# Sliding-window attention into a per-sentence expert MLP: the gate chain placed ahead of the masks, and four loads placed elsewhere in the queue

## The chip, the cores and the metric

The kernel runs on one core of a Trainium2 chip. Times are device microseconds of one execution. The kernel before was timed three times, and its median is the number to compare with. One more execution was taken by the hardware profiler, and all rows of a profile that are shown below come from it.

## The reference

```python
def reference(q, k, v, w_gate, w1, w2):          # q, k, v: 8 x 8 x 576 x 64
    scores = q @ k.T / 8                          # per batch and head, 576 x 576
    mask = (rel >= 0) & (rel < 64)                # rel = query position - key position
    attn = softmax(where(mask, scores, -1e9)) @ v
    x = attn, heads side by side                  # 8 x 576 x 512
    logits = x.mean(axis=1) @ w_gate              # 8 x 8: one row of logits per batch
    e = argmax(logits); g = softmax(logits)[e]
    out[b] = g * (relu(x[b] @ w1[e]) @ w2[e])     # w1: 512 x 1024, w2: 1024 x 512
```

Each batch (a sentence of 576 positions) picks one expert out of eight by the mean of its attention output, so the expert's weights can be fetched only when the attention of the whole batch is done.

## The kernel before, in words

The work is cut into 16 units `u`. A unit is four heads of one batch, so batch `b` has the units 2b and 2b+1. A unit passes these stages, each a helper function:

- `load_qk(u)` (L208) issues two DMAs on GpSimd's queue, which also cast q and k from float32 to bfloat16. `load_v(b)` (L219) issues v of a whole batch on SyncE's queue, behind a small GpSimd instruction.
- `transpose_qk(u, which)` (L329) transposes q (0) or k (1) on TensorE; ScalarE or VectorE copies the result out of PSUM.
- `scores(u, c)` (L366) makes a third of the score blocks on TensorE (tile `sp`). ScalarE takes exp into `pt` (L389), and VectorE multiplies `pt` by a 0/1 mask in place (L391).
- `cast_part(u, part)` (L305) copies v on VectorE: "whole" casts it to `va`, "low" and "high" copy `va`, shifted by half a block, into `vb`.
- `values(u, s)` (L398) multiplies `pt` with `va` and `vb` on TensorE (L413), and VectorE normalizes into `x` (L427, L429). It reads all three thirds of the masked `pt`.
- `transpose_x(u)` (L441) transposes `x` (L450); ScalarE copies it to `xT` and sums over positions on the way (L458). VectorE adds the gate's partial sums `gpart` (L476, L480).
- `gate(b)` (L486) is one small matmul `gl` (L488), then on VectorE `glog`, the maximum, its index and `eidx` (L492 to L500). GpSimd reads `eidx` into a register (L505), and only then can `load_w1(b)` (L526) and `load_w2(b)` (L538) be issued on its queue. `gate_weight(b)` (L510) makes the softmax weight, by which ScalarE scales `hT`.
- `expert_up(b, ft)` (L545) is one tile of x times w1 (L557), with relu on ScalarE into `hT` (L561). `expert_down(b, mt)` (L565) is a tile of hT times w2 (L571, L580), copied out on VectorE or ScalarE to `ob` and stored on SyncE's queue.

Every engine runs its instructions in the order in which the program emits them, so the order is written by hand. Units 0 to 3 are emitted one after the other (L686 to L757). From `t = 4` on, a loop (L759) runs a step for each unit: transposed x of unit t-1, scores and values of unit t, the transposes of unit t+1, and in between `experts(pace)`, which takes the next tiles of an endless list of expert tiles of earlier batches by a running budget, about eight times a step. In each even step the gate of batch t/2 - 1 is worked out by `next_gate()`: after the first `experts(pace)` in step 4, after the second in the steps 6 to 14. It issues w1, then q and k of unit t+4 (in the steps 6, 8 and 10), then w2, then v. In the odd steps `load_qk(t + 4)` is issued at the step's start.

q and k have six buffers each, w1 and w2 two each, PSUM has four buffers of two banks in one rotation, and `pt` has six.

Of the kernel before, what the change touches and what calls it, by code (L numbers as in the profile page):

```python
# [14 lines left out]
ALU = mybir.AluOpType  # L15
# [141 lines left out]
def kernel(  # L157
# [10 lines left out]
    nc = tc.nc  # L168
# [6 lines left out]
    NU = 2 * B  # L175
# [4 lines left out]
    def P(ins):  # L180
        tc.keep_in_program_order(ins)
        return ins
# [18 lines left out]
    kv = k.rearrange("b h s d -> (b h s d)").rearrange(  # L201
        "(u s r c) -> u r s c", u=NU, s=2, c=NT * D)
# [2 lines left out]

    qk_tiles = {}

    def load_qk(u):  # L208
        qn = qkn.tile([128, 2, NT * D], BF16, tag="qn")
        kn = qkn.tile([128, 2, NT * D], BF16, tag="kn")  # L210
        P(nc.gpsimd.dma_start(out=qn, in_=qv[u]))
        if u == 0:
            load_v(0)
        P(nc.gpsimd.dma_start(out=kn, in_=kv[u]))
        qk_tiles[u] = (qn, kn)

    v_tiles = {}
# [1 line left out]
    def load_v(b, behind=None):  # L219
        vn = vpool.tile([128, NM, D], FP32, tag="vn")  # L220
        if behind is None:

            P(nc.gpsimd.memset(vn[:, 0, 0:1], 0.0))
        else:

            P(nc.gpsimd.tensor_copy(out=vn[:, 0, 0:1], in_=behind))
        P(nc.sync.dma_start(out=vn, in_=vv[b]))
        v_tiles[b] = vn
# [37 lines left out]
    for (half, e, own) in ((0, 0, True), (1, 0, False), (0, 1, False), (1, 1, True)):  # L266
        sl = par[64 * half:64 * half + 64, e, :]
        if own:

            P(nc.gpsimd.affine_select(  # L270
                out=sl, in_=sl, compare_op=ALU.is_ge, fill=OUT, base=0,
                pattern=[[1, 64]], channel_multiplier=-1))
        else:

            P(nc.gpsimd.affine_select(
                out=sl, in_=sl, compare_op=ALU.is_ge, fill=OUT, base=-1,
                pattern=[[-1, 64]], channel_multiplier=1))
    outside = const.tile([128, 3, 6, 64], BF16)
    for c in range(3):
        P(nc.vector.tensor_copy(  # L280
            out=outside[:, c].rearrange("p (g e) w -> p g e w", e=2),
            in_=par[:, None, :, :].broadcast_to([128, 3, 2, 64])))
    P(nc.vector.memset(outside[64:128, 0, 0, :], OUT))
    P(nc.vector.memset(outside[0:64, 1, 3, :], OUT))
    masks = const.tile([128, 3, 2, 6, 64], FP16)
# [13 lines left out]
    def copy_on(eng, out, in_):  # L299
        if eng is nc.scalar:  # L300
            P(nc.scalar.copy(out=out, in_=in_))  # L301
        else:
            P(eng.tensor_copy(out=out, in_=in_))  # L303

    def cast_part(u, part, eng=None):  # L305
        b, qd = divmod(u, 2)
        i = b % 2
        vn = v_tiles[b]
        lo, hi = qd * HM, qd * HM + HM
        l1 = max(lo, 1)  # L310

        src = vn if eng is nc.gpsimd else va[i]
        eng = eng or nc.vector
        if part == "whole":
            copy_on(eng, va[i][:, lo:hi, 0:D], vn[:, lo:hi, :])
        elif part == "low":
            copy_on(eng, vb[i][0:64, lo:hi, 0:D], src[0:64, lo:hi, 0:D])
        else:
            copy_on(eng, vb[i][64:128, l1:hi, 0:D], src[64:128, l1 - 1:hi - 1, 0:D])

    def cast_v(u):
        for part in ("whole", "low", "high"):
            cast_part(u, part)

    qt_tiles, kt_tiles, pt_tiles, x_tiles, xt_tiles = {}, {}, {}, {}, {}
# [37 lines left out]
                rhs=outside[:, c].rearrange("p g w -> p (g w)"), start=True, stop=False))  # L363
        sp_ps[u, c] = sp

    def scores(u, c):  # L366
        qT, kT = qt_tiles[u], kt_tiles[u]
        masked = (u, c) in sp_ps
        if not masked:
            sp_ps[u, c] = psum.tile([128, 2, 512], FP32, tag="ps", name="sp")  # L370
        sp = sp_ps[u, c]

        def mm(s, half, kblk, qblk, n):
            P(nc.tensor.matmul(  # L374
                out=sp[64 * half:64 * half + 64, s,
                       64 * (qblk - 6 * c):64 * (qblk - 6 * c) + n],
                lhsT=kT[64 * s:64 * s + 64, ts(kblk, 64)],
                rhs=qT[64 * s:64 * s + 64, 64 * qblk:64 * qblk + n],
                start=not masked, stop=not masked or kblk >= g0 + 4,
                tile_position=(64 * s, 64 * half)))  # L380

        g0 = 6 * c
        for s in range(2):
            mm(s, 1, 1 if c == 0 else g0 - 1, g0, 64)
        for g in range(g0, g0 + 6):
            for s in range(2):
                mm(s, g % 2, g, g, 128 if g < g0 + 5 else 64)
        pt = ptp.tile([128, 2, 384], FP16, tag="pt")
        P(nc.scalar.activation(out=pt, in_=sp[:, :, 0:384], func=AF.Exp, scale=scale))  # L389
        if not masked:  # L390
            P(nc.vector.tensor_tensor(  # L391
                out=pt, in0=pt, in1=masks[:, c].rearrange("p s g w -> p s (g w)"),
                op=ALU.mult))
        pt_tiles[u, c] = pt

    op_ps = {}

# [37 lines left out]
    def x_chunk(b, kb):  # L435

        if b == 0:
            return slice(128 * kb, 128 * kb + 128)
        return slice(256 * (kb // 2) + kb % 2, 256 * (kb // 2 + 1), 2)

    def transpose_x(u, chunks=(0, 1), parts=True, eng=None):  # L441
        b, qd = divmod(u, 2)
        if qd == 0 and chunks[0] == 0:
            xt_tiles[b] = xtp.tile([128, KB, S], FP16, tag="xT", name=f"xT{b}")
        x, xT = x_tiles[b], xt_tiles[b]
        tp = psum.tile([128, 2, 1024], FP16, tag="ps")
        for kl in chunks:
            kb = 2 * qd + kl
            for jj in range(5):
                P(nc.tensor.transpose(  # L450
                    out=tp[:, kl, ts(jj, 128)],
                    in_=x[:, jj, x_chunk(b, kb)], identity=identh))
        for kl in chunks:
            kb = 2 * qd + kl
            if eng is not None:
                copy_on(eng, xT[:, kb, :], tp[:, kl, 0:S])
                continue
            P(nc.scalar.activation(  # L458
                out=xT[:, kb, :], in_=tp[:, kl, 0:S], func=AF.Copy,
                accum_out=pooled[:, b, kb:kb + 1]))  # L460
        if parts:
            for kl in chunks:
                gate_parts(b, 2 * qd + kl)
# [74 lines left out]
    def load_w2(b):  # L538
        P(nc.gpsimd.dma_start(
            out=weights[b][1].rearrange("p (g i) d -> p g i d", i=4),  # L540
            in_=w2e[experts_of[b]].squeeze(0)))
# [94 lines left out]
    def experts(amount):  # L636

        acc[0] += amount
        while acc[0] > 0.0:
            nxt = next(stream, None)  # L640
            if nxt is None:
                return
            nxt[0]()
            halves[0] = False
            acc[0] -= nxt[1]

            free[0] = nxt[2]

    per_step = (8 * 1.0 + 4 * 1.7 + 0.9) / 2
    START = 3  # L650
# [45 lines left out]
    for c in range(3):  # L696
        scores(0, c)
# [3 lines left out]
    leave_qk(1, 1, A)  # L701
    load_qk(3)
    load_qk(4)
    cast_v(0)
    cast_v(1)
    for c in range(3):
# [15 lines left out]
    gate(0)  # L722
    load_w1(0)
    load_w2(0)
    load_qk(5)
    load_v(2, w1_parts()[:, 0, 0, 0:1])
    load_qk(6)
    load_v(3)
# [24 lines left out]
    values(3, 1)  # L753
    transpose_qk(4, 0)
    transpose_qk(4, 1)
    experts(2.0)
    transpose_x(3)  # L757

    for t in range(START + 1, NU + LAG):  # L759
        pace = per_step / 8.0 * 0.96  # L760
        on, prev, ahead = t < NU, START + 1 < t <= NU, t + 1 < NU

        def next_gate():
            b = t // 2 - 1
            gate(b)
            load_w1(b)
            if START + 1 < t < NU - 4:
                load_qk(t + 4)
            load_w2(b)
            if t // 2 + 2 < B:  # L770
                load_v(t // 2 + 2)
            if t == START + 1:
                load_qk(7)

        for u in [8, 9] if t == 5 else [t + 4] if t % 2 == 1 else []:
            if u < NU:
                load_qk(u)
        if prev:
            transpose_x(t - 1)
        if ahead and t > 5:  # L780
            cast_part(t + 1, "whole")
        if on:
            scores(t, 0)
            scores(t, 1)
        experts(pace)
        if t == START + 1 or t == NU:
            next_gate()
        if t == NU:
            gate_weight(B - 1)
            okc = row_check()  # L790
        if ahead and t > 5:
            cast_part(t + 1, "low")
            cast_part(t + 1, "high")
        experts(pace)
        if START + 1 < t < NU and t % 2 == 0:
            next_gate()
        if on:
            scores(t, 2)
        if START < t < NU and t % 2 == 0:
            gate_weight(t // 2 - 1)  # L800
        if t == START + 1:
            cast_v(t)
        experts(pace)
        experts(pace)

        if ahead:
            transpose_qk(t + 1, 1, leave=False)
            leave_qk(t + 1, 1, free[0])
        if on:
            values(t, 0)  # L810
        halves[0] = on
        experts(pace)
        experts(pace)
        if ahead:
            transpose_qk(t + 1, 0)
        if on:
            values(t, 1)
        halves[0] = on
        if t in (4, 5):
            cast_v(t + 1)  # L820
        if t == NU:
            row_flag(okc)
        experts(pace)
        experts(pace)
# [38 lines left out]
```

## Time and profile before

| | us |
|---|---|
| median of 3 runs | 231.01 |
| lowest and highest run | 228.78, 231.4 |
| profiled execution | 227.06 |
| its span, first to last instruction | 225.2 |
| TensorE busy | 201.0 (89%) |
| VectorE busy | 128.9 (57%) |
| ScalarE busy | 134.5 (60%) |
| GpSimd busy | 37.8 (17%) |

PE is TensorE (PEld its weight loads), DVE is VectorE, ACT is ScalarE, POOL is GpSimd and SP is SyncE. A row of the timeline has the start, the duration, the engine, the line of the kernel, the operation, and output and inputs by the program's names; `x8` counts instructions merged into the row. What stands in brackets is how long the engine was idle before it, and what ended that. A row of the chain that ended last has start, duration and name alone. TensorE's idle time comes from few places: the first 14 us, in which q and k arrive, some waits in between, and the end, where the last tiles are copied and stored.

### The profile page before, as it was taken

Reading aid. Unit: us, or ns where it says so; the run is one execution under the profiler, and the core shown is the slowest. Engines: PE = TensorE matmul, PEld = TensorE weight load, DVE = VectorE, ACT = ScalarE, POOL = GpSimd, SP = SyncE. Lnnn points to the kernel's source line nnn. Section 1 sums busy time; section 2 is a strip of 40 time slices with the busy share of each in tenths; the row PEclk is TensorE's granted clock in tenths of the full one; section 3 lists DMA queues with packets and bytes.
Section 4 is the critical chain, followed back from the end, with each engine's and each line's share of the span. In section 5 each row is a group of like instructions: output and inputs, shape, how many; then the busy total and the mean of one; then the engine's idle time right before and its main releaser. Section 6 shows DMA issues by size and latency. Waiting matters only on the chain.

```text
span 225.2 us, 6993 instructions
## 1 busy us (share of the span) xinstructions
PE 201.0 (89%) x3011; PEld 142.6 (63%) x3012; DVE 128.9 (57%) x310; ACT 134.5 (60%) x220; POOL 37.8 (17%) x67
## 2 busy tenths in 40 slices
PE   7869879988799996999999998999999998999980
PEld 2436758845488655866687656865687567659630
DVE  2639695576856865575775668475948572511130
ACT  2366795962669664695769474977397457416410
POOL 7160360036000150007000610020002000200000
PEclk9979699999999999999999999999999999999996
DMA  5999899999999999998999999999941995499142
GB/s 74 241 256 248 140 187 220 245 252 221 230 234 253 274 215 237 230 271 165 225 235 243 259 212 242 234 281 205 226 147 10 184 224 175 53 223 243 74 148 69
DMA packets 29910, 45.64 MB, mean 203 GB/s; under 512 B 2480, under 2 KB 21936, under 8 KB 29872
## 3 DMA queue, kind: packets, MB, share of 16 engines
q0 software_dynamic: 13840, 26.22, 64.7%
q1 hardware_dynamic: 15232, 18.88, 27.6%
q8 instruction: 25, 0.41, 0.7%
q10 hardware_dynamic: 800, 0.03, 0.2%
q14 instruction: 13, 0.11, 0.1%
HBM read 61.90 MB, written 9.44 MB: 317 GB/s over the span
## 4 chain that ended last, share of the span: by engine, by line
PE 59%; DMA 16%; ACT 14%; DVE 4%; issue 2%; POOL 1%; POOLq 0%
PE php L557 24%; PE pso L571 18%; DMA w1t<-in_moe_w_dram 11%; PE tp L334 6%; ACT pt L389 5%; ACT xT L458 5%; DMA kn<-in_k_dram 4%; PE op L413 4%; ACT hT L561 4%; PE pso L580 2%; PE tp L450 1%; PE sp L374 1%; PE sp L361 1%; DVE vb L303 1%; DVE pt L391 1%
## 5 line engine op out<-in xcount | busy, mean ns | idle before, releaser
L557 PE MATMUL php<-xT,w1t 128*128 128x288 f16 x512 | 69.8, 287 | 5.1 <-DMA w1t<-in_moe_w_dram 4.3
L561 ACT ACTIVATE hT<-php,gatew 128x576 f16<-128x576 f32 x64 | 47.0, 745 | 31.6 <-PE php L557 31.6
L557 PEld LDWEIGHTS <-w1t 128*128 128x128 f16 x512 | 55.7, 115 | 12.6 <-DMA w1t<-in_moe_w_dram 6.0
L571 PE MATMUL pso<-w2t,hT 128*128 128x512 f16 x256 | 60.5, 380 | 1.0 <-ACT hT L561 0.9
L571 PEld LDWEIGHTS <-hT 128*128 128x128 f16 x256 | 23.3, 98 | 27.7 <-issue 1.8
L389 ACT ACTIVATE pt<-sp 128x768 f16<-128x768 f32 x48 | 36.6, 820 | 7.1 <-PE sp L374 7.1
L303 DVE COPY ob<-pso 128x512 f32<-128x512 f32 x24 | 16.5, 689 | 24.2 <-PE pso L571 24.1
L534 POOL DMA_DIRECT2D w1t<-in_moe_w_dram x7 | 5.0, 716 | 138.1 <-PE tp L334 62.8
L391 DVE TENSOR_TENSOR pt<-pt,masks 128x768 f16<-128x768 f16 x42 | 23.2, 555 | 7.5 <-ACT pt L389 6.4
L429 DVE TENSOR_TENSOR x<-op,linv 128x640 f16<-128x640 f32 x32 | 26.4, 824 | 1.1
L347 ACT COPY dst<-tp 128x1152 bf16<-128x1152 bf16 x16 | 18.0, 1122 | 14.1 <-PE tp L334 13.8
L458 ACT ACTIVATE xT<-tp 128x576 f16<-128x576 f16 x28 | 17.9, 646 | 6.2 <-PE tp L450 6.2
L413 PE MATMUL op<-vb,pt 128*64 128x65 f16 x320 | 16.0, 195 | 2.6 <-DVE vb L303 1.4
L413 PEld LDWEIGHTS <-pt 128*64 128x64 f16 x640 | 13.6, 111 | 4.8 <-issue 3.0
L374 PE MATMUL sp<-dst 64*64 64x128 bf16 (+1 forms) x672 | 14.1, 218 | 2.4 <-ACT dst L301 1.1
L413 PE MATMUL op<-va,pt 128*64 128x65 f16 x320 | 15.8, 195 | 0.0
L480 DVE SCALAR_TENSOR_TENSOR gpart<-wg,pooled,gpart 128x8 f32<-128x8 f32 x21 | 4.7, 226 | 19.3 <-ACT xT L458 19.2
L374 PEld LDWEIGHTS <-dst 64*64 64x64 bf16 x672 | 10.6, 110 | 7.5 <-issue 3.0
L427 DVE RECIPROCAL linv<-op 128x10 f32<-128x10 f32 x32 | 6.9, 217 | 14.4 <-PE op L413 14.3
L303 DVE COPY vb<-va 64x1152 f16<-64x1152 f16 (+1 forms) x32 | 14.9, 465 | 0.5
L303 DVE CAST va<-vn 128x1152 f16<-128x1152 f32 x16 | 12.4, 778 | 3.9 <-DMA vn<-in_v_dram 3.9
L334 PE MATMUL tp<-ident,kn 128*64 128x128 bf16 x288 | 11.5, 227 | 1.7 <-DMA kn<-in_k_dram 1.6
(71 smaller groups left out, 179.5 us busy)
## 6 DMA issues: line engine op xcount, KB each, us to landing
w2t<-in_moe_w_dram POOLq DMA_DIRECT2D x8, 1024.0 KB, 16.4
out_dram<-ob SPq DMA_DIRECT2D x32, 256.0 KB, 7.5
w1t<-in_moe_w_dram POOLq DMA_DIRECT2D x7, 1024.0 KB, 8.8
qn<-in_q_dram POOLq DMA_DIRECT2D x16, 288.0 KB, 13.7
kn<-in_k_dram POOLq DMA_DIRECT2D x16, 288.0 KB, 14.8
w1t<-in_moe_w_dram POOLq DMA_DIRECT2D x2, 512.0 KB, 6.4
out_dram<-ob SPq DMA_DIRECT2D x16, 64.0 KB, 7.5
vn<-in_v_dram SPq DMA_DIRECT2D x8, 0.2 KB, 19.7
```

The source lines that it names most:

```text
L303: P(eng.tensor_copy(out=out, in_=in_))
L334: P(nc.tensor.transpose(out=tp[64 * s:64 * s + 64, ts(t, 128)], in_=src[:, s, ts(t, D)], identity=ident, tile_position=(0, 64 * s)))
L347: P(nc.scalar.copy(out=dst.rearrange("p (x r t) -> p x r t", x=2, t=NT), in_=view))
L374: P(nc.tensor.matmul(out=sp[64 * half:64 * half + 64, s, 64 * (qblk - 6 * c):64 * (qblk - 6 * c) + n], lhsT=kT[64 * s:64 * s + 64, ts(kblk ...
L389: P(nc.scalar.activation(out=pt, in_=sp[:, :, 0:384], func=AF.Exp, scale=scale))
L391: P(nc.vector.tensor_tensor(out=pt, in0=pt, in1=masks[:, c].rearrange("p s g w -> p s (g w)"), op=ALU.mult))
L413: P(nc.tensor.matmul(out=op[64 * half:64 * half + 64, xx, 65 * jj:65 * jj + 65], lhsT=pt[:, s, 64 * (g % 6):64 * (g % 6) + 64], rhs=win, s ...
L429: P(nc.vector.tensor_tensor(out=x[:, :, h0 * D:(h0 + 2) * D].rearrange("p j (x c) -> p x j c", x=2), in0=view[:, :, :, 0:64], in1=li[:, :, ...
L458: P(nc.scalar.activation(out=xT[:, kb, :], in_=tp[:, kl, 0:S], func=AF.Copy, accum_out=pooled[:, b, kb:kb + 1]))
L557: P(nc.tensor.matmul(out=php[:, sc, 0:288], lhsT=w1t[:, kb, cols], rhs=xT[:, kb, ts(sc, 288)], start=(kb == 0), stop=(kb == KB - 1)))
L561: P(nc.scalar.activation(out=hT[:, ft].rearrange("p (sc s) -> p sc s", sc=2), in_=php[:, :, 0:288], func=AF.Relu, scale=gatew[:, b:b + 1]))
L571: P(nc.tensor.matmul(out=pso[:, 0, :], lhsT=hT[:, fb, ts(mt, 128)], rhs=w2t[:, fb, :], start=(fb == 0), stop=(fb == FB - 1)))
```

## The change

It has four parts.

1. In the even steps from 4 on (`gated`), `scores(t, 0)` and `scores(t, 1)` leave out the mask multiplication. The gate follows directly after the first `experts(pace)` (in step 4 ahead of it), then come the two mask multiplications (`mask_out`), and in the steps 6 to 14 the "whole" cast of the next unit's v, which stood ahead of the scores before. In step 16 the order stays as it was.
2. `transpose_x(3)` stands one expert tile earlier.
3. From step 6 on, q and k are loaded for unit t+3, no longer t+4; unit 8 is loaded in step 5 alone, and unit 9 in step 6, behind w1.
4. q of unit 5 is issued ahead of the first gate, behind q and k of unit 4. Its k stays behind w1 and w2 of batch 0.

```diff
-    def load_qk(u):
+    def load_qk(u, q=True, k=True):
+        if not q:
+            P(nc.gpsimd.dma_start(out=qk_tiles[u][1], in_=kv[u]))
+            return
...
-        P(nc.gpsimd.dma_start(out=kn, in_=kv[u]))
+        if k:
+            P(nc.gpsimd.dma_start(out=kn, in_=kv[u]))
...
-    def scores(u, c):
+    def scores(u, c, mask=True):
...
-        if not masked:
-            P(nc.vector.tensor_tensor(
-                out=pt, in0=pt, in1=masks[:, c].rearrange("p s g w -> p s (g w)"),
-                op=ALU.mult))
         pt_tiles[u, c] = pt
+        if mask and not masked:
+            mask_out(u, c)
+
+    def mask_out(u, c):
+        pt = pt_tiles[u, c]
+        P(nc.vector.tensor_tensor(
+            out=pt, in0=pt, in1=masks[:, c].rearrange("p s g w -> p s (g w)"),
+            op=ALU.mult))
...
     load_qk(4)
+    load_qk(5, k=False)
...
-    load_qk(5)
+    load_qk(5, q=False)
...
-    experts(2.0)
+    experts(1.0)
     transpose_x(3)
+    experts(1.0)
...
-            if START + 1 < t < NU - 4:
-                load_qk(t + 4)
+            if START + 1 < t < NU - 3:
+                load_qk(t + 3)
...
-        for u in [8, 9] if t == 5 else [t + 4] if t % 2 == 1 else []:
-            if u < NU:
-                load_qk(u)
+        gated = START < t <= NU and t % 2 == 0
+        if t % 2 == 1 and t + 3 < NU:
+            load_qk(t + 3)
         if prev:
             transpose_x(t - 1)
-        if ahead and t > 5:
+        if ahead and t > 5 and not gated:
             cast_part(t + 1, "whole")
         if on:
-            scores(t, 0)
-            scores(t, 1)
-        experts(pace)
-        if t == START + 1 or t == NU:
+            scores(t, 0, not gated)
+            scores(t, 1, not gated)
+        if t > START + 1:
+            experts(pace)
+        if gated:
+
             next_gate()
+            if on:
+                mask_out(t, 0)
+                mask_out(t, 1)
+        if t == START + 1:
+            experts(pace)
...
         if ahead and t > 5:
+            if gated:
+                cast_part(t + 1, "whole")
             cast_part(t + 1, "low")
             cast_part(t + 1, "high")
         experts(pace)
-        if START + 1 < t < NU and t % 2 == 0:
-            next_gate()
         if on:
             scores(t, 2)
-        if START < t < NU and t % 2 == 0:
+        if gated and on:
             gate_weight(t // 2 - 1)
```

## The prediction

> **What bounds the kernel now.** I read the page first, then what TensorE waits for, then the chain that ended last, then the order of single instructions in the even steps, because the diff touches these alone.
>
> ```profile
> span 225.2 us, 6993 instructions
> DMA  5999899999999999998999999999941995499142
> w1t<-in_moe_w_dram POOLq DMA_DIRECT2D x7, 1024.0 KB, 8.8
> kn<-in_k_dram POOLq DMA_DIRECT2D x16, 288.0 KB, 14.8
> ```
>
> The second row gives the tenths of DMA business in 40 slices: from slice 2 to about slice 30 the DMA engines hardly rest. The last two are issue rows, with KB each and the median us from issue to landing: 8.8 for w1, 14.8 for a k. In TensorE's timeline two tiles of the first expert product stand long for w1 (start, duration, in brackets the wait before):
>
> ```profile
> 60.49 1.17 PE L557 MATMUL php<-xT,w1t 128*128 128x288 f16 x8 [1.66 <-DMA w1t<-in_moe_w_dram]
> 86.37 1.17 PE L557 MATMUL php<-xT,w1t 128*128 128x288 f16 x8 [2.19 <-DMA w1t<-in_moe_w_dram]
> ```
>
> They are batches 1 and 2, loaded by the gates of steps 4 and 6. From the chain that ended last:
>
> ```profile
> 48.61 11.83 DMA w1t<-in_moe_w_dram
> ...
> 77.78 8.55 DMA w1t<-in_moe_w_dram
> ```
>
> So VectorE's gate chain (glog, max, index, eidx) sets when GpSimd may issue w1, here 48.61 and 77.78, and in these two places TensorE ends up waiting for the landing. Together that is 1.66 + 2.19 = 3.85 us, and it is what the change can win. Batch 3 shows no such wait, but it has nothing to spare:
>
> ```profile
> 110.88 2.15 PE L557 MATMUL php<-xT,w1t 128*128 128x288 f16 x16 [0.22 <-ACT pt L389]
> ```
>
> Its w1 was issued at 101.90 (row below), and 101.90 + 8.8 = 110.7.
>
> **The gate chain and the masks.** Step 8 shows how every gated step from 6 to 14 runs now:
>
> ```profile
> 96.04 2.28 PE L557 MATMUL php<-xT,w1t 128*128 128x288 f16 x16
> 97.16 0.23 DVE L480 SCALAR_TENSOR_TENSOR gpart<-wg,pooled,gpart 128x8 f32<-128x8 f32 x1 [0.40 <-ACT xT L458]
> 97.30 0.75 DVE L303 CAST va<-vn 128x1152 f16<-128x1152 f32 x1
> 97.97 1.15 DVE L391 TENSOR_TENSOR pt<-pt,masks 128x768 f16<-128x768 f16 x2
> 98.15 0.28 PE L488 MATMUL gl<-gpart,onesf 128*128 128x8 f32 x2
> 98.58 0.36 PE L374 MATMUL sp<-dst 64*64 64x64 bf16 x14
> 99.03 0.92 DVE L303 COPY vb<-va 64x1152 f16<-64x1152 f16 x2
> 99.21 1.89 PE L571 MATMUL pso<-w2t,hT 128*128 128x512 f16 x8 [0.27 <-ACT hT L561]
> 99.98 0.17 DVE L492 COPY glog<-gl 128x8 f32<-128x8 f32 x1
> 100.81 0.55 DVE L391 TENSOR_TENSOR pt<-pt,masks 128x768 f16<-128x768 f16 x1
> 101.02 0.69 PE L334 MATMUL tp<-ident,kn 128*64 128x128 bf16 x18
> 101.90 0.72 POOL L534 DMA_DIRECT2D w1t<-in_moe_w_dram  x1 [19.78 <-PE tp L334]
> ```
>
> VectorE does the cast, two masks and the vb copies (97.30 to 99.95) while the gate's sums have been ready since 97.16 + 0.23 = 97.39. After the change, TensorE's gl comes one expert tile (half of the 2.28 us row) earlier and is then held by gpart. How fast gl follows gpart, step 4 shows:
>
> ```profile
> 44.90 0.23 DVE L480 SCALAR_TENSOR_TENSOR gpart<-wg,pooled,gpart 128x8 f32<-128x8 f32 x1 [0.41 <-ACT xT L458]
> 45.27 0.36 PE L488 MATMUL gl<-gpart,onesf 128*128 128x8 f32 x2 [0.32 <-DVE gpart L480]
> ```
>
> 0.14 us, and 0.36 to its end. So gl runs 97.53 to 97.89, glog starts at 97.93, and w1 is issued 1.92 behind that (99.98 to 101.90): 99.85 instead of 101.90, 2.05 us sooner.
>
> *Step 6, batch 2.* 2.05 sooner turns 86.37 into 84.32; TensorE gets there at 86.37 - 2.19 = 84.18, plus the delay worked out next (about 0.5), so the wait is gone: 2.19 won, bounds 1.5 and 2.19. *Step 4, batch 1.* The two masks no longer stand ahead of glog (97.97 to 99.03, 1.06 us), and transpose_x(3) is moved ahead by one tile of 1.1 us, of which I count 0.7, because it may then have to wait for the norm of unit 3. That is 1.76 against a wait of 1.66: all of it won, bounds 1.06 (the masks alone) and 1.66.
>
> *What the masks cost.* The chain ends where mask 2 starts now, 0.83 behind glog: 98.76. Then come masks 0 and 1 (1.06), the cast (0.67, 97.30 to 97.97), the vb copies (0.95), and mask 2 (0.55): it ends at 101.99 instead of 101.36, 0.63 later, because VectorE idles while gl runs. Moreover the w1, q, k and w2 issues on GpSimd, 0.72 each from 99.85 on, now lie beside the cast and the copies, as in step 4 today:
>
> ```profile
> 49.68 0.95 DVE L303 CAST va<-vn 128x1152 f16<-128x1152 f32 x1 [0.35 <-DMA vn<-in_v_dram]
> 50.66 1.13 DVE L303 COPY vb<-va 64x1152 f16<-64x1152 f16 x2
> ```
>
> 0.95 and 1.13 against 0.75 and 0.92: 0.41 more. So mask 2 is 0.63 to 1.04 us late. Who waits: the value product of the same step, which follows the k transposes on TensorE. I take 0.53 us from the start of these and some 13 of 20 matmuls (0.2) before the third score block is read; that is an estimate from the 0.69 of the row, whose end overlaps with the next. Margins, step by step, mask 2 against these transposes:
>
> ```profile
> 76.41 0.55 DVE L391 TENSOR_TENSOR pt<-pt,masks 128x768 f16<-128x768 f16 x1
> 76.78 0.69 PE L334 MATMUL tp<-ident,kn 128*64 128x128 bf16 x18
> ...
> 124.81 0.55 DVE L391 TENSOR_TENSOR pt<-pt,masks 128x768 f16<-128x768 f16 x1
> 125.02 0.69 PE L334 MATMUL tp<-ident,kn 128*64 128x128 bf16 x18
> ...
> 148.82 0.55 DVE L391 TENSOR_TENSOR pt<-pt,masks 128x768 f16<-128x768 f16 x1
> 150.33 0.69 PE L334 MATMUL tp<-ident,kn 128*64 128x128 bf16 x18
> ...
> 171.83 0.55 DVE L391 TENSOR_TENSOR pt<-pt,masks 128x768 f16<-128x768 f16 x1
> 172.28 0.69 PE L334 MATMUL tp<-ident,kn 128*64 128x128 bf16 x18
> ```
>
> The slack is transposes + 0.73 - end of mask 2: 0.55 in step 6, 0.39 in steps 8 and 10, 1.69 in step 12, 0.63 in step 14. With 1.04 the new waits are 0.5 + 0.65 + 0.65 + 0 + 0.4 = 2.2 us, with 0.63 they are 0.1 + 0.25 + 0.25 + 0 + 0 = 0.6. Holding TensorE at gl costs about 0.4 a step, but what follows in step 8 waits for ScalarE anyway (0.27) and the score product after gl stood 0.15 (98.43 to 98.58), so some 0.1 a step is left: 0.4 in all over steps 4 to 14. Sum of the costs 1.0 to 2.6; I take 2.0, nearer the upper end, since the issues do fall on the casts.
>
> **The q and k loads.** One pair (2 x 288 KB) moves from ahead of w1 of batch 2 to behind it, and each later pair one step back. A step is about 12 us (half of 101.02 to 125.02), so some 24 us are left to a load, and a k lands in 14.8. I cost it at nothing: the two steps of work between issue and use hide it. Without that cover, a landing later than 24 us would hold the transposes by the rest. The DMA queue ahead of w1 gets shorter. **q of unit 5** goes into the queue right behind k of unit 4, ahead of the first gate. Its place is where the DMA engines rest (last two columns: DMA share, GB/s):
>
> ```profile
> 26.00:27.00 1.00, 1.00 (x13) 1.00 (x11) 0.65 (x3) 1.00 (x2) 0.63 (x1) 0.50 0.29 54
> 27.00:28.00 1.00, 1.00 (x27) 0.90 (x27) 0.86 (x3) 1.00 (x3) 1.00 (x3) 0.89 0.43 22
> 28.00:29.00 1.00, 0.95 (x24) 0.66 (x19) 1.00 (x3) 1.00 (x2) 1.00 (x2) 1.00 0.52 65
> ```
>
> Of 3 us 1.8 are idle. At w1's pace (1024 KB in 8.8 us, latency included) 288 KB take at most 2.5, so up to 0.7 may be left over to delay the first w1; on the other side v and k behind it may land sooner, which I bound by the same 0.7. I take 0: the rest of the transfer is hidden by the idle stretch.
>
> **The sum** on the profiled execution: 3.85 - 2.0 = 1.85 won, span 223.35; its own time was 227.06 (span + 1.86), so 225.2. The median of the runs shown is 231.01, 3.95 above that execution. What the longer runs spend is not shown. If it were late w1 for batches 3 to 7, which land with 0.2 us to spare, an issue 2 us earlier would win part of it: bounds 0 and 3.95, I take 1.0. Median after: 231.01 - 1.85 - 1.0 = **228.2 us**. A measurement of this kernel can tell about 2% (4.6 us) from no change, so this counts as within.
>
> **Rivals.** *Slower: w1's issue collides with the casts.* Where it is issued just ahead of va and vb, in step 4, it takes 11.83 to land instead of 8.8. The change puts every issue from step 6 on there. With 11.83, w1 of batch 2 lands at 77.78 - 2.05 + 11.83 = 87.6 against 84.7 (2.9 wait instead of 2.19), batch 3 at 111.7 against 111.5. Sum: -1.66 + 0.7 + 0.2 + 2.0 = +1.25, no slack won: 232.3. It ends slower from a landing time of 10.8 us on. For it: the step-4 rows. Against: that transfer also had v and q/k transfers beside it. [...]
>
> *More than forecast.* Casts aren't slowed and the slack pays: 231.01 - 3.85 + 1.0 - 2.0 = 226.2, down to 224 with all of the 3.95 bar 0.2. For it: the bare margins of batch 3. *w1 lands no sooner*, because the DMA row stays at 9 and the queue is served in order: nothing won, 0.6 of the costs hidden in the waits that stay, 231.0 + 1.4 = 232.4. Against it: fewer bytes stand ahead.
>
> **Chances.** Forecast 0.5 (226.5 to 230.5), more 0.25, collision 0.15, no sooner 0.1. Range 224 to 232.8, from the large gain to just beyond the two losses. Faster by over 2% takes less than 226.4: most of the second case and a little of the first, 0.25. Slower by over 2% takes more than 235.6, which needs collisions at several later batches as well: 0.10. Within: 0.65.
>
> **What would show it.** Right: no wait for w1 at batches 1 and 2; glog straight behind gl in steps 6 to 14; w1 issued about 2 us sooner against the step; new waits of the value product for mask 2 of 0.2 to 0.7 us in steps 6, 8, 10, 14. Wrong: w1 landings of 11 us or more in these steps (collision), waits for w1 still there, a first w1 landing later than now, or waits for q or k.

## The result, and the profile after

| | before | after |
|---|---|---|
| median of 12 runs, us | 228.90 | 226.69 |
| lowest and highest run | 228.16, 231.40 | 225.42, 230.22 |
| profiled execution, us | 227.06 | 226.77 |
| its span, us | 225.2 | 224.5 |

The ratio is 0.988, with a 95% interval from 0.983 to 0.992. It compares means, and the two longest runs of after (229.47 and 230.22), over 1.5% above its shortest, are left out as slow. The forecast of 228.2 against 231.01 was also a ratio of 0.988. So the kernel became about 2.8 us faster (1.7 to 3.9), which is within 2%. The two profiled executions differ by only 0.3 us in their own times, because that of before was shorter than all 12 timed runs of its kernel. What follows therefore reads stretches of the profiles and not their totals.

From the page of the profile of the changed kernel:

```profile
span 224.5 us, 6988 instructions
PE 200.5 (89%) x3011; PEld 141.5 (63%) x3012; DVE 129.2 (58%) x310; ACT 134.1 (60%) x220; POOL 37.9 (17%) x67
w1t<-in_moe_w_dram POOLq DMA_DIRECT2D x7, 1024.0 KB, 9.2
kn<-in_k_dram POOLq DMA_DIRECT2D x16, 288.0 KB, 12.8
```

TensorE's busy time has hardly moved (201.0 before). The gain lies in its waits. In its timeline, the first tiles of batches 0, 1 and 2:

```profile
32.90 2.15 PE L565 MATMUL php<-xT,w1t 128*128 128x288 f16 x16 [1.11 <-DMA w1t<-in_moe_w_dram]
...
60.28 1.14 PE L565 MATMUL php<-xT,w1t 128*128 128x288 f16 x8 [0.67 <-DVE ob L307]
...
84.25 1.14 PE L565 MATMUL php<-xT,w1t 128*128 128x288 f16 x8
```

Both waits for w1 that the prediction counted, 1.66 and 2.19, are gone. Batch 1 now waits 0.67 for VectorE's copy `ob`; its w1 landed at 59.75 (tile view below), 0.53 ahead of the tile. Batch 0 waits 1.11 for its w1, where the profile before has this:

```profile
31.68 2.15 PE L557 MATMUL php<-xT,w1t 128*128 128x288 f16 x16 [0.48 <-DMA w1t<-in_moe_w_dram]
```

The start of each batch's first tile cuts the span into stretches. They are the measure used below, in us from the first expert tile:

| kernel | first tile | batch 0 to 1 | 1 to 2 | 2 to 7 |
|---|---|---|---|---|
| before | 31.68 | 28.81 | 25.88 | 116.20 |
| after | 32.90 | 27.38 | 23.97 | 117.15 |
| difference | +1.22 | -1.43 | -1.91 | +0.95 |

What is left to the span's -0.7 is +0.5 behind batch 7, where I followed nothing up. A second profile of the changed kernel, further down, doesn't repeat this: its span is 223.5, its first tile starts at 32.56, and behind batch 7 it is 0.15 shorter than before.

Step 8 of the changed kernel, in the timeline:

```profile
93.97 1.17 PE L565 MATMUL php<-xT,w1t 128*128 128x288 f16 x8
95.09 0.23 DVE L488 SCALAR_TENSOR_TENSOR gpart<-wg,pooled,gpart 128x8 f32<-128x8 f32 x1 [0.41 <-ACT xT L466]
95.46 0.36 PE L496 MATMUL gl<-gpart,onesf 128*128 128x8 f32 x2 [0.32 <-DVE gpart L488]
95.86 0.17 DVE L500 COPY glog<-gl 128x8 f32<-128x8 f32 x1 [0.54 <-PE gl L496]
96.68 1.02 DVE L400 TENSOR_TENSOR pt<-pt,masks 128x768 f16<-128x768 f16 x2
97.61 0.75 DVE L307 CAST va<-vn 128x1152 f16<-128x1152 f32 x1
97.97 0.72 POOL L542 DMA_DIRECT2D w1t<-in_moe_w_dram  x1 [19.02 <-DVE pt L400]
98.40 1.28 DVE L307 COPY vb<-va 64x1152 f16<-64x1152 f16 x2
99.00 0.69 PE L338 MATMUL tp<-ident,kn 128*64 128x128 bf16 x18
99.72 0.56 DVE L400 TENSOR_TENSOR pt<-pt,masks 128x768 f16<-128x768 f16 x1
100.33 0.22 PE L421 MATMUL op<-vb,pt 128*64 128x65 f16 x1 [0.42 <-DVE pt L400]
```

The chain runs as the prediction laid it out: gl 0.14 behind gpart, glog 0.04 behind gl, w1 2.11 behind glog (1.92 before). Against the step's first expert tile w1 is issued 97.97 - 93.97 = 4.00 later. Before it was 101.90 - 96.04 = 5.86, so the issue is 1.86 us sooner (2.05 was forecast). The last row is the new wait for mask 2.

### The profile page after: what moved, and what is told of

It is laid out like the page before. It is cut to its first block, busy times and chain, and to the rows that moved or that the text cites. A ratio compares the mean times of both kernels' runs of the same rounds, so it can differ in the third digit from the quotient of the medians.

```text
span 224.5 us, 6988 instructions
## 1 busy us (share of the span) xinstructions
PE 200.5 (89%) x3011; PEld 141.5 (63%) x3012; DVE 129.2 (58%) x310; ACT 134.1 (60%) x220; POOL 37.9 (17%) x67
## 3 DMA queue, kind: packets, MB, share of 16 engines
q1 hardware_dynamic: 15232, 18.88, 27.8%
## 4 chain that ended last, share of the span: by engine, by line
PE 63%; DVE 13%; ACT 10%; DMA 7%; issue 3%; POOL 1%; POOLq 0%
PE php L565 25%; PE pso L579 20%; PE tp L338 5%; ACT xT L466 5%; DMA kn<-in_k_dram 5%; PE op L421 4%; PE pso L588 3%; DVE vb L307 3%; DMA w1t<-in_moe_w_dram 3%; DVE pt L400 2%; ACT hT L569 2%; DVE x L437 2%; PE sp L378 2%; ACT pt L393 2%; PE tp L458 2%
## 5 line engine op out<-in xcount | busy, mean ns | idle before, releaser
L579 PEld LDWEIGHTS <-hT 128*128 128x128 f16 x256 | 23.2, 98 | 25.8 <-issue 1.2
L307 DVE COPY ob<-pso 128x512 f32<-128x512 f32 x24 | 16.5, 688 | 24.4 <-PE pso L579 24.3
L351 ACT COPY dst<-tp 128x1152 bf16<-128x1152 bf16 x16 | 17.9, 1120 | 14.6 <-PE tp L338 14.2
L400 DVE TENSOR_TENSOR pt<-pt,masks 128x768 f16<-128x768 f16 x42 | 22.7, 555 | 3.9 <-ACT pt L393 2.8
L421 PE MATMUL op<-vb,pt 128*64 128x65 f16 x320 | 17.1, 195 | 3.6 <-DVE pt L400 2.0
L421 PEld LDWEIGHTS <-pt 128*64 128x64 f16 x640 | 14.2, 110 | 6.5 <-DVE pt L400 2.4
L421 PE MATMUL op<-va,pt 128*64 128x65 f16 x320 | 16.8, 196 | 0.0
L307 DVE COPY vb<-va 64x1152 f16<-64x1152 f16 (+1 forms) x32 | 16.0, 500 | 0.7
L378 PE MATMUL sp<-dst 64*64 64x128 bf16 (+1 forms) x672 | 13.6, 213 | 1.6 <-ACT dst L305 0.8
L378 PEld LDWEIGHTS <-dst 64*64 64x64 bf16 x672 | 9.8, 107 | 8.1 <-issue 4.1
```

Of the source, the lines that this page charges most:

```text
L351: P(nc.scalar.copy(out=dst.rearrange("p (x r t) -> p x r t", x=2, t=NT), in_=view))
L378: P(nc.tensor.matmul(out=sp[64 * half:64 * half + 64, s, 64 * (qblk - 6 * c):64 * (qblk - 6 * c) + n], lhsT=kT[64 * s:64 * s + 64, ts(kblk ...
L400: P(nc.vector.tensor_tensor(out=pt, in0=pt, in1=masks[:, c].rearrange("p s g w -> p s (g w)"), op=ALU.mult))
L421: P(nc.tensor.matmul(out=op[64 * half:64 * half + 64, xx, 65 * jj:65 * jj + 65], lhsT=pt[:, s, 64 * (g % 6):64 * (g % 6) + 64], rhs=win, s ...
L579: P(nc.tensor.matmul(out=pso[:, 0, :], lhsT=hT[:, fb, ts(mt, 128)], rhs=w2t[:, fb, :], start=(fb == 0), stop=(fb == FB - 1)))
```

## The experiments

Every diff is against the changed kernel. "After" and "before" are the two kernels of the case, and ratios are to before. In five of these profiles TensorE runs at half clock (granted 0.50) for some 3.5 us around the start of the first expert tile or just behind it. A star marks a stretch lengthened by this, and the last section returns to it.

**The gate order alone.** The three other parts are undone.

```diff
-    load_qk(5, k=False)
...
-    load_qk(5, q=False)
+    load_qk(5)
...
-    experts(1.0)
+    experts(2.0)
     transpose_x(3)
-    experts(1.0)
...
-                load_qk(t + 3)
+                load_qk(t + 4)
...
-        if t % 2 == 1 and t + 3 < NU:
-            load_qk(t + 3)
+        for u in [8, 9] if t == 5 else [t + 4] if t % 2 == 1 else []:
+            if u < NU:
+                load_qk(u)
```

> Only the gate chain ahead of the masks; the loads and transpose_x(3) as before. Theory (w1 is issued sooner because VectorE's chain no longer stands behind masks and casts): the wait for w1 at batch 1 shrinks from 1.66 us to 0.6 or less (transpose_x(3) is not earlier here), that at batch 2 goes; new waits of the value product for mask 2 of 0.2 to 0.5 us in steps 6, 8 and 10. Net -2 us, ratio to before 0.988 to 0.993. Rival (the shorter DMA queue ahead of w1 does it, by the later q and k): w1 is issued sooner but lands no sooner, the waits stay above 1 us each, and the new waits come on top: ratio 1.000 to 1.006.

Ratio 0.998 (0.995 to 1.0005): next to nothing, though the gate part is the core of the prediction. Stretches: batch 0 to 1 28.38, 1 to 2 25.50. In its timeline both waits for w1 are still there, in part:

```profile
61.54 1.17 PE L565 MATMUL php<-xT,w1t 128*128 128x288 f16 x8 [0.94 <-DMA w1t<-in_moe_w_dram]
...
87.04 1.17 PE L565 MATMUL php<-xT,w1t 128*128 128x288 f16 x8 [1.31 <-DMA w1t<-in_moe_w_dram]
```

Its tile views of w1 of batch 2 and of k of unit 9, the last load in the queue ahead of it (start, then us from issue to landing), say why:

```profile
L542 POOL DMA_DIRECT2D w1t<-in_moe_w_dram x1: 721/721/721, 75.9 to 75.9; - x1
DMA to landing us min/median/max: 11.1/11.1/11.1
...
L218 POOL DMA_DIRECT2D kn<-in_k_dram x1: 741/741/741, 54.0 to 54.0; - x1
DMA to landing us min/median/max: 27.6/27.6/27.6
```

w1 was issued sooner, but k of unit 9 lands only at 81.6, and w1 follows 5.4 behind it, at 87.0. In the profile before, the same k landed at 53.6 + 27.8 = 81.4 and w1 at 86.3, 4.9 behind. So w1 was issued 1.84 us sooner than before (75.94 against 77.78), and landed at nearly the same distance behind k of unit 9. As far as these two profiles show, the earlier issue only waited longer in a queue that wasn't empty yet.

**All but the gate order.** The masks go back into `scores`, the "whole" cast ahead of these, and the gate behind the second `experts(pace)`.

```diff
-        if ahead and t > 5 and not gated:
+        if ahead and t > 5:
             cast_part(t + 1, "whole")
...
-            scores(t, 0, not gated)
-            scores(t, 1, not gated)
-        if t > START + 1:
-            experts(pace)
-        if gated:
+            scores(t, 0)
+            scores(t, 1)
+        experts(pace)
+        if t == START + 1 or t == NU:
             next_gate()
...
+        if START + 1 < t < NU and t % 2 == 0:
+            next_gate()
```

> The other three parts alone: q and k three units ahead, q of unit 5 ahead of the first gate, transpose_x(3) one tile earlier; the gate chain stays behind masks and casts. Theory: w1 is issued at the same point of each step as before, so batch 2 still waits 1 us or more and batch 1 about 1 us; no wait for mask 2 in steps 6 to 10; ratio 0.995 to 1.000. Rival (the queue does it): both w1 waits are below 0.5 us and the ratio is 0.985 to 0.990, as with the whole change.

Ratio 0.9965 (0.992 to 1.001). Here the queue is short, but the issue late (77.98):

```profile
60.69 1.17 PE L565 MATMUL php<-xT,w1t 128*128 128x288 f16 x8 [1.17 <-DMA w1t<-in_moe_w_dram]
...
86.21 1.17 PE L565 MATMUL php<-xT,w1t 128*128 128x288 f16 x8 [1.83 <-DMA w1t<-in_moe_w_dram]
```

w1 of batch 2 took 8.2 us to land, less than the 8.55 of before, and 1.83 of the wait stay. So the two halves of the change come out at 0.2% and 0.35% alone, with intervals that both reach to no change, and at about 1.2% together.

**q and k four units ahead again.** The gate, q of unit 5 and transpose_x(3) stay as changed.

```diff
-                load_qk(t + 3)
+                load_qk(t + 4)
...
-        if t % 2 == 1 and t + 3 < NU:
-            load_qk(t + 3)
+        for u in [8, 9] if t == 5 else [t + 4] if t % 2 == 1 else []:
+            if u < NU:
+                load_qk(u)
```

> The changed kernel with q and k loaded four units ahead again (units 8 and 9 in step 5, ahead of the w1 of batch 2). New theory from the first four runs: the sooner issue and the shorter queue are worth nothing one by one, since w1 of batch 2 stands behind q and k of unit 9 in the queue. So w1 of batch 2 is issued as soon as in the changed kernel but lands 11 us after its issue instead of 9.2, and the wait at its first tile is 1 to 2 us; ratio 0.992 to 0.997. Rival (the sooner issue suffices, the landing follows it): landing 9 to 9.5 us, no wait, ratio 0.986 to 0.991 as the changed kernel.

Ratio 0.995 (0.993 to 0.998), but the stretch from batch 1 to 2 is 23.98, as good as after's: there is no wait for w1 at batch 2, against what was expected. Its first tile of batch 2, in the timeline:

```profile
85.10 1.14 PE L565 MATMUL php<-xT,w1t 128*128 128x288 f16 x8
```

The tile view of the same k:

```profile
L218 POOL DMA_DIRECT2D kn<-in_k_dram x1: 716/716/716, 53.8 to 53.8; - x1
DMA to landing us min/median/max: 25.3/25.3/25.3
```

It lands at 79.1, 2.5 sooner than in the first experiment, from which this kernel differs by the early q of unit 5 and transpose_x(3) alone, and w1 (issued 75.48, landing 9.2) is there at 84.7, ahead of TensorE at 85.10. The stretch from batch 0 to 1 is 28.97*. Without the 1.65 us that the half clock costs (last section) it is about 27.3, no more than after's 27.38, so this profile doesn't show what the edit loses: that the ratio fell where it was expected to fall doesn't support the reason given for it.

**Gate order and lead only.** The lead is the loading of q and k three units ahead. The two early moves, q of unit 5 and transpose_x(3), go back.

```diff
-    load_qk(5, k=False)
...
-    load_qk(5, q=False)
+    load_qk(5)
...
-    experts(1.0)
+    experts(2.0)
     transpose_x(3)
-    experts(1.0)
```

> The gate chain ahead of the masks together with q and k three units ahead; q of unit 5 and transpose_x(3) as before the change. Theory (batch 2's wait needs the sooner issue and the q and k of unit 9 out of the way, batch 1's needs the rest): from the first tile of batch 1 to that of batch 2 24.0 us as in the changed kernel (25.9 before), no wait for w1 of batch 2; gl of step 4 still waits 1.3 us for transpose_x(3); from batch 0 to batch 1 28.0 to 28.5 us. Ratio 0.990 to 0.994. Rival (q of unit 5 ahead of the first gate is what empties the queue, as the run with four units ahead suggests, where w1 of batch 2 landed in 9.2 us): landing of w1 of batch 2 10.5 us or more, wait of 1 us or more.

Ratio 0.996 (0.993 to 0.999). Batch 1 to 2 takes 23.96, again all of the gain, and the tile doesn't wait for w1:

```profile
85.56 1.14 PE L565 MATMUL php<-xT,w1t 128*128 128x288 f16 x8
```

So at batch 2 the earlier gate is needed, and with it one of two things that shorten the queue, the lead or the two early moves. In these profiles, one for each case, either suffices. Batch 0 to 1 takes 29.65*, or about 28.0 without the half clock: there the early moves are missed.

**q of unit 5 back.**

```diff
-    load_qk(5, k=False)
...
-    load_qk(5, q=False)
+    load_qk(5)
```

> The changed kernel with q of unit 5 issued behind the first w1 and w2 again. Theory (the transfer fits into the idle stretch of the DMA engines ahead of the first w1, and nothing downstream waits for it): first half of w1 of batch 0 lands 5.3 us after its issue as before, and the time is that of the changed kernel within 0.3%: ratio 0.985 to 0.991. Rival (q of unit 5 delays the first w1, which landed 5.8 us after its issue in the changed kernel's profile, with a wait of 1.1 us instead of 0.5): 0.5 us faster than the changed kernel and the wait at the first expert tile back at 0.5. Second rival (it shortens the queue ahead of w1 of batch 1): the wait for w1 at batch 1 comes back with 0.5 us or more.

Ratio 0.992 (0.988 to 0.995). Batch 1 is where it differs, 28.04 against 27.38. But its first tile starts 0.92 sooner (31.98), so that batch 1 begins at 60.02, hardly sooner than the 60.28 of after. Its timeline:

```profile
60.02 1.17 PE L565 MATMUL php<-xT,w1t 128*128 128x288 f16 x8 [1.25 <-DVE gpart L488]
```

The bracket names gpart. Yet this kernel's tile view of w1 of batch 1 has

```profile
L542 POOL DMA_DIRECT2D w1t<-in_moe_w_dram x1: 713/713/713, 47.0 to 47.0; - x1
DMA to landing us min/median/max: 12.9/12.9/12.9
```

which is a landing at 59.92, 0.1 ahead of the tile: it waited for w1. After the change the issue is 0.93 later and the landing is not, 47.95 + 11.8 = 59.75. The tile view of after:

```profile
L542 POOL DMA_DIRECT2D w1t<-in_moe_w_dram x1: 716/716/716, 47.9 to 47.9; - x1
DMA to landing us min/median/max: 11.8/11.8/11.8
```

**transpose_x(3) back.**

```diff
-    experts(1.0)
+    experts(2.0)
     transpose_x(3)
-    experts(1.0)
```

> The changed kernel with transpose_x(3) behind both expert tiles again. Theory (in step 4 the sums of unit 3 are what gl waits for, once it no longer stands behind a tile): gl's wait in step 4 is 1.3 us instead of 0.4, w1 of batch 1 is issued 0.7 to 1 us later against the first expert tile (15.05 us behind it in the changed kernel), and the kernel is 0.5 to 1 us slower than the changed one: ratio 0.990 to 0.994. Rival (w1 of batch 1 is late by the transfers beside it and not by its issue): same landing, ratio as the changed kernel, 0.986 to 0.990.

Ratio 0.993 (0.989 to 0.997). In step 4 gl now stands for gpart 1.33 us, 0.37 after the change:

```profile
49.09 0.39 PE L496 MATMUL gl<-gpart,onesf 128*128 128x8 f32 x2 [1.33 <-DVE gpart L488]
```

The interval overlaps with after's, and batch 0 to 1 (29.38*) is lengthened by the clock, so this part is worth up to about 0.5%, and not surely anything. Its tile view of w1 of batch 1 tells more:

```profile
L542 POOL DMA_DIRECT2D w1t<-in_moe_w_dram x1: 716/716/716, 51.4 to 51.4; - x1
DMA to landing us min/median/max: 9.1/9.1/9.1
```

Issued 3.4 us later than in after, it lands only 0.7 later, at 60.5. The first kernel with late casts below agrees: issued at 50.09, w1 lands in 9.5. Counted from the issue of the first w1 (which itself lies anywhere from 26.1 to 27.7), the landing of w1 of batch 1 falls at 32.6 to 33.5 us in the ten profiles with q of unit 5 early (mean 32.9) and at 33.3 to 34.1 in the four with it late (mean 33.7), while its issue falls anywhere from 20.4 to 24.4. So here the landing hardly follows the issue.

**v of batch 3 behind w1 of batch 1**, to find what that transfer waits for.

```diff
-    load_v(3)
...
             load_w1(b)
+            if t == START + 1:
+                load_v(3)
```

> The changed kernel with v of batch 3 issued in step 4 behind the w1 of batch 1, no longer before step 4. Question: why w1 of batch 1 takes 11.8 us to land in both kernels, where the other gates need 8 to 9.7. Theory (v of batch 3 keeps the DMA engines until it is through): landing 8 to 10 us after the issue, and the wait at batch 1's first tile is left to the eviction that is late there (0.7). Rival (the casts on VectorE beside GpSimd's issue, as in the slower case of the prediction): landing stays at 11.5 us or more. The time isn't the question: v comes later, and VectorE may wait for it in step 5.

Ratio 0.998 (0.994 to 1.001). w1 landed in 9.2 us, as the theory of a queue ahead wanted. But its issue came late here (50.91), and at such an issue w1 lands in 9.1 with v in its old place too (row above). So the run doesn't tell v from the rest of the queue. That v is what holds w1 of batch 1 stays argued, not shown. Batch 1 to 2 takes 26.08 here, 2.1 us more than in after. v of batch 3 came 1.03 late for its cast, but that is not what TensorE waited for:

```profile
86.89 0.69 DVE L307 COPY ob<-pso 128x512 f32<-128x512 f32 x1 [2.97 <-DMA out_dram<-ob]
87.64 1.89 PE L579 MATMUL pso<-w2t,hT 128*128 128x512 f16 x8 [1.98 <-DVE ob L307]
```

The copy waits for a store to leave its buffer. On SyncE's queue the first stores follow the two issues of v at 68.45, in after at 52.10. So, as far as this profile shows, late stores cost it these 2 us.

**The casts behind mask 2**, in the gated steps.

```diff
-        if ahead and t > 5:
-            if gated:
-                cast_part(t + 1, "whole")
+        if ahead and t > 5 and not gated:
...
             gate_weight(t // 2 - 1)
+        if ahead and t > 5 and gated:
+            cast_v(t + 1)
```

> The changed kernel with the cast of the next unit's v and its two vb copies moved behind mask 2 in the even steps from 6 on (ahead of the k transposes in program order). Theory (mask 2 is late because the cast and the copies stand ahead of it): the waits of the value product for mask 2 in steps 6, 8 and 10 (0.2, 0.4, 0.4 us in the changed kernel's profile) go to 0, ratio to before 0.981 to 0.985, that is 1 us less than the changed kernel. Rival (VectorE's work only moves the wait: the norms and the evictions behind the casts come late and PSUM's four buffers hold TensorE): new waits of TensorE for norm or eviction of 0.3 us or more in those steps, ratio 0.986 to 0.992.

Ratio 0.989 (0.983 to 0.995), no different from after's. The waits for mask 2 in the even steps are gone (the 1.07 of step 11 stays), batch 1 to 2 is 23.63 (0.34 less), 2 to 7 116.81 (0.34 less). But in step 12 the late casts push the normalization, and the second product waits for it:

```profile
150.80 1.90 PE L579 MATMUL pso<-w2t,hT 128*128 128x512 f16 x8 [0.89 <-DVE x L437]
```

**The casts behind mask 2 in every step from 6 on**, and those of step 4 at its end; run twice.

```diff
-        if ahead and t > 5:
-            if gated:
-                cast_part(t + 1, "whole")
-            cast_part(t + 1, "low")
-            cast_part(t + 1, "high")
         experts(pace)
         if on:
             scores(t, 2)
...
+        if ahead and t > 5:
+            if gated:
+                cast_part(t + 1, "whole")
+            cast_part(t + 1, "low")
+            cast_part(t + 1, "high")
...
-        if t in (4, 5):
+        if t == 5:
             cast_v(t + 1)
...
+        if t == 4:
+            cast_v(t + 1)
```

> The changed kernel with every cast of the next unit's v made later: from step 6 on behind mask 2 and the tiles after it, in odd steps too (there only the vb copies), and in step 4 at the step's end. Theory (VectorE's order is what still stops TensorE: mask 2 in steps 6 to 11, the eviction ahead of batch 1): the waits for mask 2, 2.0 us in the changed kernel, and the 0.7 us for the eviction go; ratio to before 0.975 to 0.983. Rival (the waits move to norms, PSUM buffers and w1): ratio 0.984 to 0.990, with new waits of 1 us or more in all.

> The kernel with the late casts once more, beside the one with the empty matmuls and for a narrower interval: ratio 0.978 to 0.984. If the half clock behind the first expert tile belongs to this program, it shows again in the profile (batch 0 to batch 1 28.3 us); if it is chance, this profile may show 26.7.

Ratios 0.982 (0.977 to 0.987) and 0.983 (0.977 to 0.989). Batch 2 to 7 takes 115.46 in both, 1.69 less than after. After's waits of TensorE:

```profile
PE gl L496 <- DVE gpart L488: 2.8, 7, 0.8
PE op L421 <- DVE pt L400: 2.0, 4, 1.1
```

and those of the second of these runs (us in all, times, longest):

```profile
PE gl L496 <- DVE gpart L488: 2.8, 7, 0.8
PE php L565 <- DMA w1t<-in_moe_w_dram: 1.6, 1, 1.6
PE pso L579 <- DVE x L437: 0.9, 1, 0.9
```

In the second the value product no longer waits for a mask at all: not for the 0.88 us that the change brought, nor for the 1.07 of step 11, which the kernel before had too. The price is the 0.9 for the normalization.

**The changed kernel again**, for a second profile.

> The changed kernel as it is, for the comparison on the same chip and for a second profile: ratio 0.985 to 0.991; no wait for w1 at batch 2, 0 to 0.7 us at batch 1; waits for mask 2 of 0.2 to 0.4 us in steps 6, 8, 10. If instead the first profile was lucky, a wait for w1 of 0.5 us or more shows at one of the batches 1 to 4.

Ratio 0.990 (0.985 to 0.994); stretches 27.38, 23.96 and 117.12, within 0.03 of after's. The late casts are to be compared with this ratio: 0.982 against 0.990, and their intervals overlap a little (0.985 to 0.987).

**Late casts, and matmuls on idle data** (ten more) ahead of and behind the scores of unit 3, where TensorE otherwise idles for the first w1 (2.10 and 1.58 us in the two profiles of the late casts). The diff shows only what is added to the late casts of above.

```diff
-    busy(3)
+    busy(7)
     for c in range(3):
         scores(3, c)
+    busy(6)
```

> The kernel with the late casts, with four more empty matmuls ahead of the scores of unit 3 and six behind them, so that TensorE isn't idle for some 2 of the 3 us ahead of the first expert tile. In three of nine profiles (the kernel with four units ahead, that with the late casts, and that with v of batch 3 moved) TensorE ran some 3.5 us at half clock right behind that wait, which cost 1.6 us. Theory (the idle stretch brings the low clock): granted clock 1.00 from 30 us on, batch 0 to batch 1 some 26.7 us, ratio 0.975 to 0.980, runs closer together. Rival (the low clock comes whenever it comes, or the empty matmuls hold the first expert tile): a low clock after 30 us again, or first expert tile later than 33.4; ratio 0.980 to 0.986.

Ratio 0.978 (0.973 to 0.984), the lowest of all. Its interval overlaps with those of the late casts alone (median 223.75 against 224.46), so the late casts are shown to beat before, and the matmuls are not shown to add to that.

## Why the prediction was right, point by point

**The waits for w1 are won: right in sum, wrong in its reasoning.** Forecast 3.85; measured 1.43 + 1.91 = 3.34, new costs inside these stretches included. The step that failed is "2.05 sooner turns 86.37 into 84.32", which lets the landing follow the issue. The gate order alone brought the issue forward, and the wait for w1 at batch 2 shrank from 2.19 to 1.31 and not to nothing, with a landing 5.4 us behind the last k in the queue. The rival "w1 lands no sooner" has the mechanism of that one part (in the profile before, all 49 loads of GpSimd's queue land in the order of their issue), though not its time: 232.4 stands for 0.6% slower, and the part came out at 0.998. The whole change escaped it through its other parts.

**q and k three units ahead, at nothing: the wrong account.** They were costed as loads that might come late. They are one of the two things that let batch 2's gain through; the prediction says that the queue ahead of w1 gets shorter and gives that no price.

**q of unit 5, at 0 between bounds of 0.7: right as a net, by two effects that cancel.** It delays the first w1, whose first half lands 5.3 to 5.4 us after its issue in the four profiles with q late, and 5.4 to 7.3 in the ten with q early (5.8 in after). That is the "first w1 landing later than now" which the prediction lists as a sign of being wrong. In return w1 of batch 1 lands 33.7 - 32.9 = 0.8 sooner against the first w1's issue. Taken out, it left 0.992 against 0.988 and 0.990, and the intervals overlap.

**transpose_x(3), 0.7:** the 0.96 less of gl's wait in step 4 is of that size, but without it w1 of batch 1, issued 3.4 us later, landed only 0.7 later, so it was not worth this in w1.

**The masks' cost, 2.0: mis-sized.** In step 8 mask 2 ends 7.43 us behind the start of the step's transpose_x instead of 6.44, 0.99 later; in the other steps from 6 to 14 it is 0.81 to 0.94 later. All of this lies between the 0.63 and 1.04 forecast. The vb copies take 1.28 in step 8 and 1.11 in the others (forecast 1.13), and the cast isn't slowed (0.75, forecast 0.95). But the waits of the value product are 0.22, 0.42, 0.24, 0 and 0 in steps 6 to 14: 0.88, where the upper bound had 2.2. The term that was too small is the slack. In step 8 the value product's own turn came at 100.33 - 0.42 = 99.91, 0.91 behind the start of the k transposes. The estimate was 0.73, of which 0.2 was for the matmuls ahead of the third score block; these take 0.38 (from 99.53 on). The hold at gl, 0.32 a step, is paid back almost whole by the waits for `hT` (0.27 to 0.36) that stood there before. From batch 2 on the stretch is 0.95 longer, and step 6 costs about 0.2 to 0.3: some 1.2 in all.

**The slack of the longer runs, 1.0: not shown.** It was to be late w1 at batches 3 to 7. No profile of the changed kernel or of before shows such a wait; one of 0.20 at batch 5 (all but the gate order) is the only one of all. No long run of the kernel before was profiled, though. What does go with the longer runs is the clock: of the 61 runs of the kernel before on which the comparisons with the experiments rest, the shortest 15 average 227.3 us at a mean granted clock of 0.983, the longest 15 229.6 at 0.973. That is a correlation, and the cause of the longer runs stays open. The measured 1.7 to 3.9 us contain the 1.85 of the profiled sum with or without the slack. That forecast and result agree to 0.001 is therefore in part luck. By the stretches, 3.34 less 0.95 from batch 2 on gives 2.4, but the first tile comes 1.22 later in one profile of the changed kernel and 0.88 in the other, so that their spans are only 0.7 and 1.7 shorter than that of before. What the 12 runs gained beyond this stays open.

**The collision rival: refuted.** In the steps 6 to 14 w1 is issued beside the cast or just ahead of it, and its landings are 8.0 to 9.7, 9.2 in the median row against 8.8 before; the rival needed 10.8. With the casts behind mask 2 the cast of step 8 begins 1.63 us behind w1's issue (98.91 against 97.28), in after 0.36 ahead of it, and w1 of the batches 2 and 3 lands in 8.2 to 10.4 in the profiles of the kernels with late casts (9.3 in the mean of seven landings), in the mean no sooner than in after, where it is 9.2 at both. The 11.8 at step 4 falls to 9.1 when the same transfer is issued 3.4 us later, and is 9.2 with v of batch 3 behind w1, where the cast starts 2.6 us behind w1's issue as it does in after. So these landings don't show that the casts hold up w1. Its issue on GpSimd takes 0.72 to 0.75 us as against 0.71 to 0.72 before, and it is the vb copies that got slower, from 0.92 to 1.11 and 1.28.

## What to carry to other kernels

An earlier issue need not bring an earlier landing. With the gate order alone w1 of batch 2 was issued 1.84 us sooner than before, and landed 5.4 us behind the last k ahead of it, where it had been 4.9. That was 11.1 us behind its issue; in the thirteen other profiles it landed 8.2 to 9.9 behind it. Look at the landing of the last load ahead before you count an earlier issue as won, and test such edits together, since each alone may show nothing. When a chain is moved ahead on an engine, look at who reads the work that it displaces: here moving the casts as well took another 1.7 us off the stretch from batch 2 to 7.

## What was not expected of the hardware

TensorE's granted clock fell to half (0.50) at places that differ from profile to profile, for about 3.5 us (3.4 in after, from 25.8 to 29.2) or, in windows between 12 and 22 us, for up to twice that (6.8 in the gate order alone, from 14.2 to 21.0). Five of the fourteen profiles have it somewhere between 32 and 39 us, on the first expert tiles. In the profile of gate order and lead only, the first 16 matmuls take 3.34 us instead of 2.15, and the windows (two us each; the last three columns are clock, DMA share and GB/s) read:

```profile
31.95 3.34 PE L565 MATMUL php<-xT,w1t 128*128 128x288 f16 x16 [0.83 <-DMA w1t<-in_moe_w_dram]
...
32.00:34.00 2.00, 2.00 (x12) 1.51 (x13) 1.66 (x4) 1.69 (x3) 1.72 (x4) 0.68 1.26 211
34.00:36.00 2.00, 2.00 (x27) 1.21 (x26) 0.00 (x0) 0.82 (x2) 0.00 (x0) 0.50 1.10 220
```

The same windows with matmuls on idle data:

```profile
32.00:34.00 2.00, 2.00 (x13) 1.27 (x12) 1.75 (x5) 1.92 (x3) 1.30 (x3) 1.00 1.22 203
34.00:36.00 2.00, 2.00 (x34) 1.64 (x33) 0.73 (x2) 1.41 (x2) 0.75 (x2) 1.00 1.17 221
```

The price is 1.65 us: the kernel with late casts was profiled twice, and its stretch from batch 0 to 1 is 28.30 with the drop and 26.65 without. It explains the starred stretches. The wait for w1 at that place was 0.83 to 2.73 us in the five, and waits of 1.1 to 1.6 in other profiles went without a drop. What brings the drop stays open. The profile with idle matmuls has none either, but nor has the second one of late casts without them, so one profile doesn't show that they prevent it.
